# A written-out order of 5993 steps, replaced by another: RWKV-7 attention into a SwiGLU block on one Trainium2 core

## Chip, cores, metric

The kernel runs on one core of one Trainium2 chip. The metric is the device time of one launch in microseconds (us). A core has these engines, each with a queue of its own that it works through in order: TensorE (in the profile PE for matmuls and PEld for the loading of the stationary operand), VectorE (DVE), ScalarE (ACT), GpSimd (POOL; here it mostly issues DMAs) and SyncE (SP; it issues DMAs). Matmuls write to PSUM, and DVE and ACT read it out.

## What is computed

The first half is a recurrence over 768 time steps, for 4 batches of 8 heads with a state of 40 x 40 each; the second half takes its output as 3072 tokens of 320 numbers through a normalisation and a gated feed-forward block with 1536 hidden columns. The feed-forward weights come as 64-bit floats; the kernel works in fp32.

```python
for t in range(S):                                   # S = 768, per batch and head
    y[t] = r[t] @ state
    Sa = state @ a[t]
    state = state * w[t][:, None] - outer(Sa, b[t]) + outer(v[t], k[t])
x = y rearranged to (B*S, H*D)                       # 3072 x 320
xn = x / sqrt(mean(x*x) + 1e-6) * rms_g
g = xn @ w_gate
out = ((g * sigmoid(g)) * (xn @ w_val)) @ w_out
```

## The kernel before

**Stages.** The sequence is cut into 24 chunks of 32 time steps; a chunk is worked on for all 32 batch-heads at once. Each chunk c has three parts, and the feed-forward block has a fourth, for groups of chunks (GROUPS, L21: one chunk, eleven times two, one chunk).

- `front(c)` (L643): loads w, a, k, b and v of the chunk, turns them on PE against the identity (two "turn" steps, L618), and builds, level by level (1, 2, 4, 8, 16), the products of keys with decays. Its PE steps are four "gramk" steps (L683 and, for the levels 4, 8 and 16, L706); between them DVE and ACT prepare the next level's K and Ab. One "turnS" follows.
- `inverse(c)` (L757): solves a triangular system on DVE, with small operations on the tiles Yi and tmp, between two trips through DRAM (sB and sY, issued by SP).
- `main(c)` (L794): PE steps "state", "lower" (two to four), "update", "turn", "turnS", "score", "y0" and five "level" steps, with DVE and ACT between them; then the normalisation with "turn4" and "turn3". It carries the state from chunk to chunk.
- `feed(g)` (L930): for each pair of the 12 slices of the hidden columns, "h64" and "hh" products (gate and value), SiLU on ACT into sg, a multiplication on DVE into hT, and an "out" product into the tile po. The weights come as slices; `narrow` (L964) turns each half slice from 64-bit floats into fp32, with integer and floating operations on DVE and ACT, numbered 0 to 23 in the order of the slices. Slices from the third on are loaded by POOL.

**Operations in the profile.** All operations are recorded by helpers, so the profile's lines are the helpers': L469 is every matmul, L472 every turn on PE, L423 nearly every DVE operation, L450, L453 and L446 the ACT copies, scalings and functions, L466 every DMA, L462 a fill by POOL. What an operation belongs to is read from its tiles' names: `ps` is PSUM but for `po`, `KN` the levels' keys, `As` the scores, `xg` the feed's input, `wf` its weights.

**The order.** The code above does not run in its own order. `Plan.add` (L241) records 5993 steps: 2717 for DVE, 1113 for ACT, 1091 for PE (a step of PE is a whole group of matmuls, for instance the 32 of one "gramk"), 588 for POOL and 484 for SP, each with what it reads and writes. `Plan.issue` (L282) then issues them in one total order, which stands in the literal `ORDER` (L32). Each number there is a distance from the first step not issued yet:

```python
for word in order.split():
    i = first + int(word)
    gone.add(i)
    while first in gone:
        first += 1
```

So the order on each engine's queue is that of its steps in this list. A second literal, `PAIRS` (L185), gives each of 495 "rooms" one of three tiles of PSUM, of two banks each (`ps0` to `ps2`). A room is one use of such a tile, from the first matmul that writes it to the last operation that reads it out (`Plan.room`, L216); a tile is held by one room at a time. The fourth pair of banks, `po`, is not part of this. Before an operation runs, semaphores make it wait for what it needs on other engines; those waits follow from the tiles that it reads and writes.

**Shapes on PE.** A step's stationary operand has rows and columns, which the profile shows as rows*columns in front of the shape of what is moved. The steps differ in them: 128*128 for "hh" and "out", 64*128, 64*104 or 40*128 for "h64" and the turns, 128*40 for "level", 64*64 down to 64*40 for "gramk", "score", "y0" and "update", 64*32 for "state", 32*32 or 16*32 for "lower".

Of the kernel before, what the change touches and what calls it, by code (L numbers as in the profile page):

```python
# [32 lines left out]
76 84 83 86 75 71 2 3 4 5 6 7 0 35 47 0 17 54 64 0 0 51 0 35 0 55 0 0 67 68 60 190 191 41 49 374 59 71 375 0  # L33
35 0 0 0 46 359 380 185 73 0 32 170 171 181 75 74 73 0 1 27 3 0 368 2 0 352 373 343 173 2 167 166 342 72 80 73 85 84 96 69
70 78 83 94 74 365 79 40 53 353 62 371 61 366 354 64 51 52 374 54 81 15 93 75 82 76 92 95 91 367 86 89 90 63 183 77 100 344 168 39
165 297 298 88 104 184 102 106 97 87 105 101 198 108 98 107 348 345 103 185 190 113 99 346 16 656 668 175 176 9 5 31 109 112 368 355 369 116 114 117
115 118 120 119 110 111 347 186 187 122 356 299 359 349 203 370 350 191 657 18 665 4 357 188 197 284 19 17 28 375 121 71 196 376 667 666 43 382 285 377
358 123 202 379 201 213 30 0 401 171 652 41 199 359 379 198 360 25 191 123 300 299 210 124 125 126 127 213 128 211 301 129 192 130 209 203 131 193 132 221
208 206 402 392 654 391 382 390 205 133 207 134 181 657 170 5 194 377 223 219 135 222 136 214 217 137 218 138 204 216 230 393 139 380 225 411 140 141 215 410
413 142 143 226 144 145 383 146 147 148 149 150 151 224 412 234 663 384 235 236 152 385 386 237 168 387 153 155 662 154 156 394 388 403 389 407 395 404 238 239  # L40
240 396 180 414 415 405 406 6 43 318 7 13 433 22 408 398 676 157 432 179 418 399 419 241 416 397 409 229 188 158 159 160 161 400 228 417 452 31 453 244
420 441 443 245 246 434 247 248 444 677 227 242 435 436 243 442 249 220 250 251 252 438 253 254 464 463 169 437 285 454 461 0 460 253 254 437 255 453 284 256
438 456 454 285 286 287 257 482 0 250 251 435 643 447 252 436 449 473 283 280 253 254 281 450 282 255 223 493 256 439 257 258 259 260 261 494 651 437 292 455
438 262 22 662 263 264 440 293 441 456 661 660 1 296 475 457 483 459 479 284 303 458 482 299 460 298 484 285 300 485 461 297 648 665 476 304 302 306 305 222
307 309 477 301 495 310 502 505 650 503 478 664 499 311 221 313 312 266 267 265 268 270 314 504 23 315 486 496 497 763 316 480 271 269 272 764 317 822 821 481
487 498 832 819 676 500 318 488 506 319 490 320 766 544 489 663 501 669 491 507 321 767 322 545 833 768 769 770 536 508 535 829 670 677 323 492 675 682 771 820
525 324 671 772 775 510 680 681 773 692 668 774 534 524 509 325 778 679 678 693 690 688 672 686 765 689 691 673 687 683 779 828 533 16 2 831 827 674 294 699
694 697 511 700 512 526 701 824 830 834 649 823 295 698 702 703 685 527 528 705 684 546 695 782 838 658 0 204 370 380 211 378 203 511 333 205 212 215 206 216
389 390 391 228 467 463 462 460 382 213 381 459 465 464 475 476 214 221 398 222 470 385 383 457 458 388 392 395 393 394 466 461 224 384 469 386 223 217 225 471
450 468 474 752 230 451 226 399 400 401 402 403 404 405 406 407 408 409 410 751 499 249 749 762 759 411 472 412 387 413 473 414 517 250 761 513 415 477 518 416  # L50
417 478 760 418 419 479 420 421 480 422 423 481 424 425 426 427 482 614 615 516 617 510 227 229 509 750 428 629 515 514 396 520 429 431 430 630 432 528 521 397
526 527 522 532 530 529 533 534 523 544 524 531 537 536 541 525 542 538 540 535 543 539 436 434 545 549 553 548 0 553 549 434 545 555 432 550 560 546 554 556
565 566 567 551 558 250 557 230 234 235 518 254 255 231 232 251 617 564 568 571 570 765 615 618 619 233 252 236 559 620 253 770 621 453 569 256 574 771 259 630
257 623 258 260 757 499 575 576 577 578 579 580 581 582 583 584 585 586 587 588 589 590 591 592 593 594 595 596 622 625 624 626 627 597 598 454 746 632 634 633
747 269 764 635 631 0 637 481 0 1 0 478 399 669 679 668 515 558 565 555 516 177 670 556 517 518 519 400 401 181 520 671 178 402 672 564 522 523 521 524
563 562 574 557 477 566 182 179 180 403 567 183 561 568 560 559 573 572 569 570 571 575 576 577 578 579 783 184 844 854 842 841 843 784 682 744 684 685 528 525
526 840 678 852 527 786 683 186 580 187 689 479 404 697 488 407 406 489 696 787 188 788 789 688 690 702 190 849 848 857 405 700 785 713 851 853 839 191 189 701
581 695 790 710 858 791 582 192 850 712 691 583 698 795 584 711 794 724 193 733 709 792 699 847 793 585 692 194 708 798 196 707 693 799 703 195 706 694 723 717
714 719 722 718 704 705 725 715 721 730 0 725 585 715 733 5 196 6 719 734 7 730 726 1 727 736 0 733 6 198 799 0 194 0 547 798 46 799 194 805
0 730 796 543 719 47 728 190 192 803 729 722 798 42 731 799 806 43 44 801 805 48 49 802 795 797 804 50 807 0 763 0 763 689 690 691 692 693 694 695  # L60
767 765 764 766 686 696 768 697 1067 769 803 687 698 770 0 943 942 694 800 766 695 799 767 41 1075 696 802 697 805 1064 698 48 47 813 806 803 1065 1063 1073 699
818 700 817 42 43 0 768 767 1030 657 757 0 4 769 770 784 657 762 5 658 774 0 779 658 762 770 780 775 46 782 791 778 659 781 660 763 776 661 53 52
47 49 54 0 43 759 657 772 784 658 769 659 779 783 788 660 782 661 787 790 662 45 785 664 663 781 50 780 789 791 684 794 665 0 687 746 754 749 639 975
752 753 755 45 0 702 41 424 52 967 42 59 0 572 4 5 710 708 15 382 1 709 384 6 10 7 711 11 383 714 0 10 15 780 11 16 0 573 571 572
570 591 796 799 798 592 780 931 913 717 712 719 713 714 721 715 716 723 718 720 0 0 0 766 781 630 767 914 907 904 631 706 709 710 0 767 905 682 768 0
619 709 710 711 712 713 714 715 716 717 718 719 720 721 722 1 364 894 768 3 769 0 0 1 408 405 341 406 0 356 357 405 358 359 235 311 360 0 414 235
3 360 415 361 236 362 237 363 364 238 365 418 366 367 0 367 428 368 419 394 369 1 430 418 370 238 371 0 0 368 427 0 0 414 418 419 417 421 415 416
423 420 426 430 367 368 543 369 427 431 428 544 545 429 724 370 371 0 431 738 306 432 728 371 538 433 732 434 0 371 434 720 372 538 0 731 434 372 373 0
734 550 537 373 2 376 374 375 377 378 0 718 554 541 2 720 3 542 537 565 727 553 4 725 311 6 547 548 715 730 551 543 312 550 726 552 576 555 563 562
716 560 561 558 723 564 559 7 557 570 544 8 379 9 545 575 380 571 574 13 546 595 378 569 556 566 577 567 568 12 578 584 572 585 582 0 581 9 576 10  # L70
582 5 568 0 568 577 572 383 217 6 579 219 384 569 581 422 578 12 423 220 580 424 654 218 652 425 520 426 653 14 509 655 8 656 585 7 586 587 588 590
589 13 9 591 592 427 593 657 594 595 0 654 591 593 655 594 5 653 10 595 596 597 598 599 600 601 602 603 604 605 606 607 608 609 610 388 658 389 611 577
659 12 578 662 673 663 664 675 668 612 669 665 613 666 667 614 670 671 13 18 14 19 615 676 682 15 20 616 617 618 16 619 620 621 674 672 989 622 677 623
678 680 681 624 679 625 626 982 992 991 979 980 505 981 683 627 628 684 514 629 0 0 0 4 613 668 614 669 615 670 671 616 617 702 706 842 703 575 704 618
619 620 717 707 716 621 709 6 12 722 710 622 624 715 711 623 705 721 719 718 7 733 729 727 744 712 720 731 843 625 728 723 725 730 9 732 713 738 726 13
8 743 14 714 742 737 739 626 734 749 724 10 629 627 745 15 735 639 736 746 748 740 755 747 763 754 756 0 0 962 678 688 741 697 629 742 617 833 661 395
398 397 749 746 748 662 396 747 0 0 657 681 943 954 814 815 658 961 724 829 830 951 828 953 659 626 734 962 671 393 817 0 951 626 817 1 943 398 3 820
# [969 lines left out]
```

## Time and profile before

| what | value |
|---|---|
| median of the runs shown | 1012.67 us (3 runs, 1006.22 to 1016.76) |
| span of the profiled execution | 1021.8 us |
| mean granted TensorE clock over that span | 0.943 |
| HBM read and written | 55.05 MB and 10.22 MB |

The span runs from the first to the last instruction of the profiled execution, and it is that execution's time as far as the profile tells. How to read the lines below: busy time of an engine and its share of the span; "in 40 slices" means tenths of each slice of 25.5 us; a chain is followed back from the last instruction to what released it. A timeline row has the start, the time to the end of the last of its instructions, engine, line, operation, out<-in, rows*columns, shape and count, and in brackets the engine's idle time before it and who ended it. A row of a group has the count, then the busy time in us and the mean of one in ns, then the idle time before them. One fp32 matmul is two records of PE; a turn is one. Ends of matmuls are modelled, so times between steps of PE are taken from start to start.

### The profile page before, as it was taken

What the parts mean: (1) busy time and instruction counts of PE and PEld (TensorE: products, weight loads), DVE (VectorE), ACT (ScalarE), POOL (GpSimd) and SP (SyncE); (2) the same over time, 40 slices, a digit from 0 to 9 for tenths busy, and PEclk for the clock granted to TensorE, in tenths of its full rate; (3) what the DMA queues carried; (4) which work ended last, traced back from release to release, by engine and by line L of the source; (5) the groups of instructions that cost most, each with busy time, mean ns of one, the idle gap of its engine ahead of it and who ended that gap; (6) DMA issues with size and microseconds to landing.
All of it is one profiled execution on the core that took longest, in us unless ns stands there. A gap on an engine that the chain in (4) does not pass through costs nothing.

```text
span 1021.8 us, 55373 instructions
## 1 busy us (share of the span) xinstructions
PE 930.1 (91%) x24512; PEld 759.6 (74%) x24512; DVE 771.4 (75%) x2718; ACT 509.7 (50%) x1133; POOL 350.0 (34%) x595
## 2 busy tenths in 40 slices
PE   4366688999989999999999999999999999999998
PEld 4255577878767787788788777778787878788877
DVE  8889877787867966877769779679598697685531
ACT  6788467445445544465353454454544545435121
POOL 8988363242324314315133143143133224210000
PEclk9557767999999999999999999999999999999999
DMA  8574453323324324133232142242232323320100
GB/s 172 149 190 115 96 110 74 68 47 60 54 58 78 56 53 75 36 71 61 45 81 44 44 95 39 55 84 49 43 72 51 75 50 66 67 35 7 43 8 20
DMA packets 140175, 68.87 MB, mean 67 GB/s; under 512 B 120768, under 2 KB 127264, under 8 KB 139936
## 3 DMA queue, kind: packets, MB, share of 16 engines
q0 software_dynamic: 19680, 32.48, 15.9%
q1 hardware_dynamic: 118080, 32.54, 15.4%
q8 instruction: 192, 3.15, 1.3%
q10 hardware_dynamic: 2176, 0.33, 0.2%
q14 instruction: 47, 0.39, 0.1%
HBM read 55.05 MB, written 10.22 MB: 64 GB/s over the span
## 4 chain that ended last, share of the span: by engine, by line
PE 55%; DVE 24%; DMA 7%; issue 5%; POOL 4%; ACT 3%; SPq 2%; DVEq 0%; ACTq 0%; POOLq 0%
PE ps L469 40%; PE po L469 10%; PE ps L472 5%; DVE Yi L423 4%; DVE LT L423 3%; DVE y L423 3%; DVE tmp L423 3%; DVE K L423 3%; DMA sB<-LT 3%; SPq L466 2%; DVE As L423 2%; DMA M<-sB 2%; DVE Ab L423 1%; POOL wf L466 1%; DVE hT L423 1%
## 5 line engine op out<-in xcount | busy, mean ns | idle before, releaser
L469 PE MATMUL ps<-xg,wf 128*128 128x256 f32 (+3 forms) x1872 | 364.5, 377 | 1.5 <-ACT sg L446 0.8
L469 PEld LDWEIGHTS ps<-xg,wf 128*128 128x128 f32 (+1 forms) x1872 | 271.1, 191 | 48.6 <-issue 8.1
L469 PE MATMUL po<-wf,hT 128*128 128x320 f32 x576 | 179.0, 444 | 0.2 <-issue 0.2
L469 PEld LDWEIGHTS po<-wf,hT 128*128 128x128 f32 x576 | 103.5, 189 | 35.6 <-issue 1.4
L423 DVE TENSOR_TENSOR tmp<-Yi,M 128x24 f32<-128x24 f32 (+21 forms) x512 | 107.2, 209 | 12.1 <-DMA M<-sB 1.6
L423 DVE TENSOR_TENSOR Yi<-Yi,tmp 128x24 f32<-128x24 f32 (+21 forms) x512 | 106.8, 209 | 10.4
L423 DVE TENSOR_TENSOR hT<-ps,sg 128x256 f32<-128x256 f32 (+1 forms) x156 | 60.6, 399 | 63.7 <-PE ps L469 41.4
L446 ACT ACTIVATE sg<-ps 128x256 f32<-128x256 f32 (+1 forms) x156 | 54.5, 368 | 103.3 <-PE ps L469 102.4
L466 POOL DMA_DIRECT2D kbn<-in_k_dram x92 | 53.6, 585 | 146.9 <-PE ps L469 146.2
L466 POOL DMA_DIRECT2D kbn<-in_b_dram x92 | 53.8, 587 | 131.2 <-PE ps L469 130.1
L423 DVE TENSOR_TENSOR K<-K,T 128x256 f32<-128x256 f32 (+1 forms) x191 | 92.8, 499 | 3.7 <-PE ps L469 2.8
L469 PE MATMUL ps<-Ab,K 64*60 64x56 f32 (+2 forms) x4608 | 79.4, 224 | 17.5 <-ACT r L450 4.8
L469 PEld LDWEIGHTS ps<-Ab,K 64*60 64x60 f32 (+2 forms) x4608 | 72.6, 136 | 29.0 <-issue 9.3
L423 DVE SCALAR_TENSOR_TENSOR Yi<-M,Yi 128x31 f32<-128x31 f32 (+6 forms) x228 | 43.2, 243 | 66.7 <-DMA out_dram<-o 23.3
L450 ACT COPY KN<-ps 128x640 f32<-128x640 f32 x95 | 65.6, 692 | 46.7 <-PE ps L472 12.9
L466 POOL DMA_DIRECT2D VU<-in_v_dram x92 | 54.1, 590 | 88.0 <-PE ps L469 86.3
L423 DVE TENSOR_TENSOR As<-ps,msi 128x256 f32<-128x256 f32 (+1 forms) x168 | 70.7, 455 | 11.9 <-PE ps L469 7.0
L469 PEld LDWEIGHTS ps<-As,KN 128*40 128x40 f32 x3072 | 67.3, 128 | 15.2 <-issue 5.3
L469 PE MATMUL ps<-As,KN 128*40 128x32 f32 x3072 | 72.0, 208 | 6.1 <-DVE As L423 2.9
L466 POOL DMA_DIRECT2D wn<-in_w_dram x92 | 52.4, 571 | 69.6 <-DVE KN L423 65.4
L450 ACT COPY K<-K 128x512 f32<-128x512 f32 x95 | 60.2, 634 | 23.7 <-PE ps L469 10.9
L456 POOL TENSOR_TENSOR ss<-ss,mhalf 128x1 f32<-128x1 f32 x24 | 18.1, 755 | 147.1 <-DVE ss L423 146.9
(137 smaller groups left out, 1526.4 us busy)
## 6 DMA issues: line engine op xcount, KB each, us to landing
M<-sB SPq DMA_DIRECT2D x96, 128.0 KB, 2.9
wan<-in_r_dram SPq DMA_DIRECT2D x24, 160.0 KB, 4.2
kbn<-in_b_dram POOLq DMA_DIRECT2D x92, 40.0 KB, 2.5
VU<-in_v_dram POOLq DMA_DIRECT2D x92, 40.0 KB, 2.7
wan<-in_w_dram POOLq DMA_DIRECT2D x46, 80.0 KB, 3.0
wan<-in_a_dram POOLq DMA_DIRECT2D x46, 80.0 KB, 2.8
kbn<-in_k_dram POOLq DMA_DIRECT2D x92, 40.0 KB, 2.7
wn<-in_w_dram POOLq DMA_DIRECT2D x92, 40.0 KB, 2.9
```

Source lines behind the costliest of these rows:

```text
L423: plan.add("DVE", time + more + each * size(o), 0.087, lambda at: [fn(at(o), *m(at))], [o], aps(*args))
L446: scalar(o, [a], lambda at: nc.scalar.activation(at(o), at(a), f, **kw), aps(acc), 0.1 if f in (AF.Square, AF.Relu) else 0.0)
L450: scalar(o, [a], lambda at: nc.scalar.copy(at(o), at(a)), extra=more)
L456: plan.add("POOL", 0.5, 0.06, lambda at: nc.gpsimd.tensor_tensor(o, a, b, op), [o], [a, b])
L466: plan.add(by, 0.6 if by == "POOL" else 0.45, 0.0, lambda at: queue.dma_start(out=o, in_=i), [o], [i], load=load, since=since)
L469: return o, lhsT, rhs, lambda at: nc.tensor.matmul(at(o), lhsT, rhs, start=start, stop=stop, skip_group_check=True), 4
L472: return o, i, ident, lambda at: nc.tensor.transpose(at(o), i, ident), 2
```

## The change

Only the two literals change. Nothing in the code that records or issues steps changes, so the 5993 steps, their instructions, and what they read and write are the same; what differs is the total order of the steps, and which of the three PSUM tiles each room uses.

```diff
 ORDER = """
-76 84 83 86 75 71 2 3 4 5 6 7 0 35 47 0 17 54 64 0 0 51 0 35 0 55 0 0 67 68 60 190 191 41 49 374 59 71 375 0
...
 PAIRS = """
-212020210212120201011000000002122102121202002110201212101120120100121021022021021012211022112120021122201112110120220200
...
-112220222120210
+012020211110110202122012002002221020200121110112220101221201120110010221222020001211121110112102011120212121001220012122
...
+000112121012120
```

Taken as indices into the recorded steps, the two lists compare like this:

| engine | steps | mean shift of a step's place in its queue | largest |
|---|---|---|---|
| PE | 1091 | 3.6 | 25 |
| DVE | 2717 | 7.0 | 175 |
| ACT | 1113 | 5.0 | 37 |
| POOL | 588 | 9.5 | 98 |
| SP | 484 | 3.8 | 35 |

The first nine steps of PE are the same; after them the lists part. Before, PE goes on with the first product of `main(0)`, the four "gramk" of `front(1)`, a turn of `front(2)`, and then the rest of `main(0)`. After, `front(1)` goes first, then `main(0)` up to its first "level" steps, and that turn of `front(2)` stands among them. The feed of group 0 begins with the 90th step of PE before, and with the 93rd after; there, before, the four "gramk" of `front(4)` stand together ahead of it.

More of the change, by code (lines that the diff above doesn't have):

```diff
@@ L32 @@
 ORDER = """
[150 rows of a table removed]
[150 rows of a table added]
 """
 PAIRS = """
-212020210212120201011000000002122102121202002110201212101120120100121021022021021012211022112120021122201112110120220200
-211101012202202011120000200020220222022111222002110010201111111221020101112100110011110120101220200212221202210202000120
-200001010122101111022221020102022012211212111120001012110101122002220000222011120101011110101020010100212121202001201010
-202022202022012001121220211222122020022201202021101121220111201111101001012220112210102111212102000010100200202021210201
-112220222120210
+012020211110110202122012002002221020200121110112220101221201120110010221222020001211121110112102011120212121001220012122
+110000102110020222200202111100101120121200020101000120101022212021211112100022021222222202020002100021000010201201001202
+022111111210120202010201212212202120120212111120101202121010022201010100021122221212022210121000210100200201020112021121
+112011002020100012212101010020201112021112010122010002020121212111000220221001102010221022221102200201020011221211012021
+000112121012120
 """
```

299 rows, old and new, of the table ORDER are left out of this document.

## The prediction

> **What bounds the kernel now.** I read the busy rows and slices first, then stretches of the span, then the chain, then PE's own timeline.
>
> ```profile
> span 1021.8 us, 55373 instructions
> PE 930.1 (91%) x24512; PEld 759.6 (74%) x24512; DVE 771.4 (75%) x2718; ACT 509.7 (50%) x1133; POOL 350.0 (34%) x595
> PE   4366688999989999999999999999999999999998
> DVE  8889877787867966877769779679598697685531
> PE 55%; DVE 24%; DMA 7%; issue 5%; POOL 4%; ACT 3%; SPq 2%; DVEq 0%; ACTq 0%; POOLq 0%
> ```
>
> PE is nearly full from the tenth slice on; in the slices before that DVE is the fuller one. So there are two stages with different limits. The place where one hands over to the other is the last of front(5)'s four level products, the second half of this group:
>
> ```profile
> 192.09 0.28 DVE L423 TENSOR_TENSOR Ab<-Ab,T 128x128 f32<-128x128 f32 x1
> 192.16 1.83 PE L469 MATMUL ps<-Ab,K 64*56 64x56 f32 x128
> ```
>
> The stretches, cut there and finer (PE, PEld, DVE, ACT, POOL busy, then granted clock):
>
> ```profile
> 0.00:50.00 50.00, 20.15 (x672) 18.25 (x672) 44.49 (x138) 33.40 (x60) 44.58 (x83) 0.78 0.72 160
> 50.00:100.00 50.00, 31.93 (x1288) 28.55 (x1288) 44.40 (x127) 41.04 (x78) 44.01 (x71) 0.64 0.64 154
> 100.00:150.00 50.00, 35.53 (x1314) 32.22 (x1315) 41.51 (x138) 29.51 (x62) 23.45 (x40) 0.64 0.47 105
> 150.00:200.00 50.00, 45.07 (x1445) 39.34 (x1429) 39.15 (x129) 30.26 (x70) 16.86 (x29) 0.89 0.34 66
> 0.00:193.20 193.20, 125.90 (x4541) 112.65 (x4545) 166.23 (x521) 131.59 (x262) 126.62 (x217) 0.73 0.55 123
> 193.20:1022.00 828.80, 804.24 (x19989) 646.93 (x19978) 605.15 (x2197) 378.10 (x871) 223.39 (x378) 0.99 0.28 54
> ```
>
> The reader is to see: in the first 193.20 us DVE works 166.23, PE only 125.90. In the other 828.80 us PE works 804.24, and DVE has 223 us of slack. So the time is, nearly, DVE's work ahead of the handover plus PE's work behind it, plus 27.0 us of idle DVE in the first stretch and 24.6 us of idle PE in the second. An order changes the two sums only by moving steps across the handover and by changing what PE loses between steps; the rest of its effect is in the 27.0 and the 24.6.
>
> **The change, part by part.** No instruction is added or removed; I took each number of the two lists as an index into the 5993 steps, and counted.
>
> *Changes of shape.* By shape I mean a stationary operand's rows*columns, each rounded up to 32, 64 or 128. The old list has 487 changes of shape between matmuls that follow each other, the new one 471. Behind the handover: 422 against 408, of which 156 against 144 enter 128*128 (hh and out), 155 against 143 leave it, and 111 against 121 are others. So 12 visits to 128*128 fewer, 10 other changes more. Their price is in PE's timeline:
>
> ```profile
> 403.30 1.13 PE L469 MATMUL ps<-xg,wf 128*128 128x256 f32 x4
> 404.36 0.78 PE L469 MATMUL ps<-ST,aP 64*32 64x40 f32 x64
> 416.74 0.20 PE L469 MATMUL ps<-r,Sd 64*40 64x32 f32 x2
> 416.76 0.20 PE L469 MATMUL ps<-rE,Sd 64*40 64x32 f32 x1
> 416.89 0.54 PE L469 MATMUL po<-wf,hT 128*128 128x320 f32 x1
> 447.03 3.72 PE L469 MATMUL ps<-xg,wf 128*128 128x256 f32 x16
> 450.68 0.79 PE L469 MATMUL ps<-Xs,LT 32*32 32x40 f32 x64
> ```
>
> One hh step (x4) holds PE from 403.30 to 404.36, 1.06 us; four in a row from 447.03 to 450.68, 3.65. So a further step costs (3.65 - 1.06) / 3 = 0.863 and the visit itself 1.06 - 0.863 = 0.197. To that comes the entry: 416.76 to 416.89 is 0.13, where matmuls of one shape follow after 0.02; 0.11 more. A visit costs 0.31 us, another change about 0.11 (I take the entry gap for it). Sum: -12 x 0.31 + 10 x 0.11 = -2.6 us. The lower end is nothing where PE would have stood still anyway, 24.6 of 828.8, so 3% of it; the upper is -3.7 if the ten others cost nothing. The two changes saved ahead of the handover count as nothing: DVE covers them. Cover gone, they cost two times 0.11.
>
> The Trainium skill, in TensorEngine Tiling (Array Packing), Key Properties, says that a change of tiling mode, not of tile alone, drains the engine. By that rule alone all changes cost alike: -14 x 0.11 = -1.5 us. The rows agree that a change costs, and differ in that a visit to 128*128 costs more than two gaps (0.31 against 0.22); I go by the rows.
>
> *Steps moved over the handover, DVE.* 516 of DVE's steps stood up to the one that releases that product, now 513. Out go three of narrow 23, KN2 of front(4) and one T; in come one hT and one Yi.
>
> ```profile
> L423 DVE TENSOR_SCALAR o<-exs 128x480 int32<-128x480 int32 x2 | 0.8, 402 | 0.0
> L423 DVE TENSOR_SCALAR exs<-exs 128x480 int32<-128x480 int32 x2 | 0.8, 398 | 0.0
> L423 DVE SCALAR_TENSOR_TENSOR exs<-exs 128x480 f32<-128x480 uint32 x2 | 1.3, 646 | 0.0
> L423 DVE TENSOR_TENSOR KN<-kbn,wn 128x640 f32<-128x640 f32 x24 | 19.7, 821 | 0.8 <-issue 0.5
> L423 DVE TENSOR_TENSOR T<-T 128x16 f32<-128x16 f32 x22 | 3.7, 168 | 0.1
> L423 DVE TENSOR_TENSOR hT<-ps,sg 128x128 f32<-128x128 f32 x24 | 6.5, 288 | 24.6 <-PE ps L469 15.1 <-ACT sg L446 8.1 <-PE po L469 1.4
> L423 DVE TENSOR_TENSOR Yi<-Yi,tmp 128x8 f32<-128x8 f32 x24 | 4.1, 169 | 0.2
> ```
>
> 0.402 + 0.398 + 0.646 + 0.821 + 0.168 - 0.288 - 0.169 = 2.0 us less. What is put off runs in DVE's slack behind the handover; without that slack it would cost the same 2.0 there. Ends: 0 if the moved steps only make idle time, and the 27.0 us of idle DVE either way if the stage packs better or worse.
>
> *Steps moved over the handover, PE.* One: the update of main(3), behind it before, now ahead, where PE is idle a third of the time. Its like:
>
> ```profile
> 430.45 0.83 PE L469 MATMUL ps<-VU,KN 64*40 64x40 f32 x64
> 431.22 0.75 PE L472 MATMUL ps<-ident,kbn 64*104 64x64 f32 x16
> ```
>
> 430.45 to 431.22, less one exit gap of 0.13: -0.64 us. If DVE did not cover it there, it would cost the same 0.64.
>
> *The queues.* On POOL, the loads for front(2)'s second turn now end with the 93rd of POOL's steps, not the 77th; on PE that turn is 23rd, not 16th.
>
> ```profile
> 50.69 1.10 PE L472 MATMUL ps<-ident,kbn 64*104 64x64 f32 x16 [8.25 <-POOL kbn L462]
> 86.09 1.97 PE L469 MATMUL ps<-A,K 64*64 64x56 f32 x64
> L466 POOL DMA_DIRECT2D kbn<-in_k_dram x92 | 53.6, 585 | 146.9 <-PE ps L469 146.2
> ```
>
> Sixteen steps at 0.585 make 9.4 us later; what reads that turn's result first is PE's product at 86.09, 35 us after it, so I cost it at nothing; with the cover gone it would be 9.4. Behind that turn on PE stood, idle for 8.25 us, the work of chunk 0; in the new list seven of these steps go first. SP's 484 loads shift by 3.8 places in the mean, and SP's queue has 2% of the chain: nothing, at most that 2%, 20 us, either way.
>
> *PSUM pairs.* Behind the handover 113 of 413 rooms followed their pair's last writing step after less than 2 us of PE work; now 135 of 412. Price nothing, since PE's idle time there is small; its end is in the second rival.
>
> **Sum.** -2.6 - 2.0 - 0.6 = -5.2 us: 1016.6 against the profiled 1021.8. The runs shown have a median of 1012.67 (1006.22 to 1016.76), 0.9% under the profiled span; scaled, 1007.5 us. Bounds of these terms alone: 1003 to 1012. About 1%, 10 us, is what a measurement of this kernel can tell from no change.
>
> **The rivals.**
>
> *Faster: chunk 0 no longer stands behind that turn.* All 8.25 us go on to the end: 1007.5 - 8.2 = 999.3. It decides (over 1%) from 5 us of the 8.25. For it: only 137 instead of 205 of DVE's steps stand ahead of main(1)'s first product. Against it: DVE, which bounds this stage, was busy 44.40 of those 50 us, so there were 5.6 us to win there, and steps that come sooner in one place come later in another.
>
> *Slower: the PSUM pairs come round too soon.* 22 more rooms have less than 2 us of cover. A reader that empties a pair takes
>
> ```profile
> L450 ACT COPY KN<-ps 128x640 f32<-128x640 f32 x95 | 65.6, 692 | 46.7 <-PE ps L472 12.9
> ```
>
> and if PE waits out such a copy in each, 22 x 0.692 = 15.2 us: 1007.5 + 15.2 = 1022.7. It passes 1% from 0.7 us each. Against it: the 113 of before cannot have cost over 24.6 us in all, 0.22 each, and 22 x 0.22 is 4.8, still within 1%. For it: PE has no slack behind the handover, so a wait of any kind there shows whole.
>
> *Slower: the granted clock.* It was 0.64 in 50:150 and 0.89 in 150:200. If the new order leaves PE's first-stage work in thinner groups and the clock stays at half, the work of 150:200 grows by 45.07 x (0.89 / 0.5 - 1) = 35 us; with half of it on the path, 1007.5 + 17 = 1025. Against it: DVE's work up to the handover and PE's are as before, to 2 us and one step, so PE is as dense there as it was. The Trainium skill, in TensorE: Matmul & The Clock Gate, Part 1, has the clock at half until a window of steady work lets it up; 0.64 between 50 and 150 and 0.99 behind 193 agree.
>
> *The change does little of what it says.* 16 changes fewer of 487 is 3%. That is in the forecast: even at 0.31 us each they would be worth 5 us.
>
> **How the numbers follow.** The forecast, within 1%, gets 0.44. Both sums are counted, but 52 us of idle time that a new order deals out anew are not. Faster gets 0.30: one place with a long wait is visibly mended, in a stage with little to win. Slower by PSUM gets 0.22, by the clock 0.04. So faster 0.30, same 0.44, slower 0.26. The likeliest gives 1007.5, its own range 1002 to 1013; the range for 8 in 10 takes in 999 with as much again of the idle 27 (988) and 1022.7 to 1025: 988 to 1026.
>
> **What would show it.** Right: PE behind the handover busy some 2 to 4 us less, DVE about 164 us ahead of front(5)'s last product, that product near 191, PE's idle time behind it near 25 us. The first wait of 8.25 us on POOL's kbn gone or short. Wrong: the handover off by over 8 us (the first stage packs otherwise), or idle PE behind it over 35 or under 15 us. A single hh visit not near 1.06 us against 0.863 for a further step would make the price wrong.

## The result, and the profile after

| | median | runs | ratio to before |
|---|---|---|---|
| before | 1011.76 us | 4 runs, 1006.22 to 1016.76 | |
| after | 1037.79 us | 4 runs, 1034.85 to 1045.08 | 1.0267, 95% interval 1.0215 to 1.0320 |

The change makes the kernel 26 us slower. 1007.5 was forecast, and 988 to 1026 as the range: the time lies outside it. The profiled execution of before (span 1021.8) lies 1% above its median, that of after (1034.5) a little under its own, so the two profiles differ by 12.7 us only; a second profiled execution of before, below, has 1017.4.

The page of after, the lines that answer to those of before:

```profile
span 1034.5 us, 55331 instructions
PE 926.7 (90%) x24512; PEld 765.0 (74%) x24512; DVE 781.9 (76%) x2718; ACT 509.2 (49%) x1133; POOL 346.0 (33%) x595
PE   5356678999999998999989999899999999999998
DVE  8987977786877886868878778688687787686541
PE 67%; DVE 11%; issue 8%; DMA 5%; ACT 4%; POOL 3%; SPq 2%; DVEq 0%; POOLq 0%; ACTq 0%
```

PE's busy time fell by 3.4 us, and yet the span grew. In the chain, "issue" (time in which an engine waits for nothing that the profile shows) went from 5% to 8%, and PE's slices show eights where before had nines. The stretches, cut at the handover of after (the last gramk of front(5), now at 195.64):

```profile
0.00:195.70 195.70, 125.52 (x4594) 112.43 (x4598) 167.39 (x517) 130.64 (x258) 120.84 (x214) 0.73 0.53 122
195.70:1034.00 838.30, 801.14 (x19936) 652.58 (x19924) 614.56 (x2203) 378.51 (x875) 225.18 (x381) 0.99 0.27 54
```

Behind the handover PE works 801.14 us, 3.1 less than in the first profile of before, as forecast; but the second profile of before has 801.52, so two executions of one kernel differ by as much:

```profile
193.20:1017.40 824.20, 801.52 (x20010) 644.91 (x20001) 605.54 (x2198) 378.50 (x871) 223.38 (x378) 1.00 0.28 55
```

What grew is the time in which PE stands idle there: 838.30 - 801.14 = 37.2 us, where before has 24.6. What it waits for is in the waits of PE from 196 us on (us in all, times, longest), first before, then after:

```profile
PE ps L469 <- issue: 6.4, 8, 2.3
```

```profile
PE ps L469 <- issue: 23.6, 27, 1.8
PE ps L469 <- DMA LT<-sY: 4.2, 3, 2.9
PE ps L472 <- issue: 2.4, 2, 1.7
```

So in 29 of its waits, 26.0 of the 37.2 us, no operand, no PSUM tile and no engine is late as far as the profile shows. PE's waits for other engines even became fewer: all that stand in the same list with ACT or DVE as the releaser come to 10.0 us before and to 2.2 after. Two of the 29 places in the timeline of after, the updates of main(9) and main(10):

```profile
440.31 1.33 PE L469 MATMUL ps<-Ab,K 64*56 64x56 f32 x92
441.46 0.31 PE L469 MATMUL ps<-VU,KN 64*40 64x40 f32 x11
443.37 0.73 PE L469 MATMUL ps<-VU,KN 64*40 64x40 f32 x53 [1.60 <-issue]
444.03 1.34 PE L469 MATMUL po<-wf,hT 128*128 128x320 f32 x4
445.31 1.13 PE L469 MATMUL ps<-xg,wf 64*128 64x256 f32 x8
...
479.60 2.86 PE L469 MATMUL ps<-xg,wf 128*128 128x256 f32 x12
482.39 1.83 PE L469 MATMUL ps<-Ab,K 64*56 64x56 f32 x128
484.04 0.31 PE L469 MATMUL ps<-VU,KN 64*40 64x40 f32 x10
486.20 0.74 PE L469 MATMUL ps<-VU,KN 64*40 64x40 f32 x54 [1.85 <-issue]
```

The update of main(9) is the row at 430.45 that the prediction quoted from before: 0.77 us to the next step there, 444.03 - 441.46 = 2.57 here. The pause cuts the step in two, after 11 of 64 records in one place and 10 in the other.

Counting PE's instructions from its first (each matmul record, each weight load, each semaphore event as one), the pause at 443.37 stands ahead of number 84 x 256 + 193. So do most others: behind the handover 29 gaps in which no matmul runs are over 0.35 us, and 24 of them lie at 192 or 193 beyond a multiple of 256, 24.7 of 29.7 us. Counted from one matmul's start to the next (over 0.35 us, less 0.1 us each for the matmul itself), 36 lie at 190 to 197, 32.0 us in all; before it is 15 with 9.8 us. This second count is the one used below. The page shows what has that period. This row of the DMA queues is the same before and after:

```profile
q8 instruction: 192, 3.15, 1.3%
```

3.15 MB in 192 packets, 16 KB each, for 24512 + 24512 matmuls and loads: 255 a packet. The runs below, which add instructions to PE alone, have one packet more for every 256 of them (193 in e5 with 24640 matmuls, 194 in e17 with 24782; 35 in e4 with 4480). So PE's instructions come by DMA, in blocks of 256.

### The profile page after: what moved, and what is told of

The parts are those of the page before. It is cut to its first block, busy times and chain, and to the rows that moved or that the text cites. A ratio compares the mean times of both kernels' runs of the same rounds, so it can differ in the third digit from the quotient of the medians.

```text
span 1034.5 us, 55331 instructions
## 1 busy us (share of the span) xinstructions
PE 926.7 (90%) x24512; PEld 765.0 (74%) x24512; DVE 781.9 (76%) x2718; ACT 509.2 (49%) x1133; POOL 346.0 (33%) x595
## 3 DMA queue, kind: packets, MB, share of 16 engines
q8 instruction: 192, 3.15, 1.3%
## 4 chain that ended last, share of the span: by engine, by line
PE 67%; DVE 11%; issue 8%; DMA 5%; ACT 4%; POOL 3%; SPq 2%; DVEq 0%; POOLq 0%; ACTq 0%
PE ps L469 49%; PE po L469 13%; PE ps L472 6%; SPq L466 2%; DVE y L423 2%; DVE Yi L423 1%; DVE tmp L423 1%; DMA wf<-in_moe_w_out_dram 1%; ACT VU L450 1%; DVE As L423 1%; DVE LT L423 1%; DVE K L423 1%; DMA sB<-LT 1%; DVE wf L423 1%; DMA LT<-sY 1%
## 5 line engine op out<-in xcount | busy, mean ns | idle before, releaser
L469 PEld LDWEIGHTS po<-wf,hT 128*128 128x128 f32 x576 | 105.9, 193 | 37.7 <-issue 3.4
L450 ACT COPY K<-K 128x512 f32<-128x512 f32 x95 | 60.3, 635 | 31.2 <-PE ps L469 14.1
L423 DVE SCALAR_TENSOR_TENSOR Yi<-M,Yi 128x31 f32<-128x31 f32 (+7 forms) x228 | 46.1, 244 | 36.4 <-DMA M<-sB 17.1
```

The costliest lines, as they stand in the source:

```text
L423: plan.add("DVE", time + more + each * size(o), 0.087, lambda at: [fn(at(o), *m(at))], [o], aps(*args))
L450: scalar(o, [a], lambda at: nc.scalar.copy(at(o), at(a)), extra=more)
L469: return o, lhsT, rhs, lambda at: nc.tensor.matmul(at(o), lhsT, rhs, start=start, stop=stop, skip_group_check=True), 4
```

## The experiments

**Theory F:** at each cut between two blocks PE stands still unless the block before took long enough, some 3.3 us. Steps of small matmuls in a row (gramk, gramk, update; state, lower, lower) use up 256 instructions in 1.5 to 2 us. Whether a cut falls behind such a run is settled by the number of instructions ahead of it, which the forecast did not look at; the change moved the cuts. **Rival O:** the new order has waits of its own between steps, and "issue" is only their name. Behind each ratio below (4 to 12 runs each) stands its 95% interval; "+ 256" is 256 more instructions of PE; "issue" is the sum of PE's waits of that name over the whole span, from the profile.

| kernel | ratio to before | issue, us (times) | span |
|---|---|---|---|
| before, first and second profile | | 10.4 (14), 10.5 (12) | 1021.8, 1017.4 |
| before + 256 ahead (e5) | 1.0013 (0.998 to 1.0046) | 9.9 (12) | 1021.7 |
| before + 176 ahead (e1) | 1.0245 (1.0191 to 1.030) | 28.0 (35) | 1035.4 |
| before + 96 ahead (e2) | 1.0287 (1.0253 to 1.0321) | 39.4 (41) | 1048.9 |
| before + 176 at 230 us (e9) | 1.0267 (1.0225 to 1.0309) | 31.2 (34) | 1044.0 |
| before + 256 at 230 us (e10) | 1.0051 (1.0021 to 1.0082) | 6.5 (11) | 1019.2 |
| the same, own outputs (e18) | 1.0042 (1.0014 to 1.007) | 8.6 (10) | 1016.3 |
| before + 32 at 800 us (e12) | 1.0000 (0.9973 to 1.0028) | 6.7 (11) | 1015.1 |
| before, feed steps spread (e7) | 1.0109 (1.0074 to 1.0143) | 9.9 (13) | 1032.2 |
| after | 1.0267 (1.0215 to 1.032) | 33.9 (38) | 1034.5 |
| after + 96 ahead (e3) | 1.0275 (1.0218 to 1.0331) | 34.3 (31) | 1038.7 |
| after, feed steps spread (e6) | 1.0292 (1.0228 to 1.0355) | 22.4 (28) | 1047.0 |
| after, cuts moved at 2 places (e11) | 1.0204 (1.0163 to 1.0246) | 20.1 (28) | 1032.5 |
| at 9 places (e13) | 1.0220 (1.0182 to 1.0258) | 17.3 (21) | 1034.7 |
| at 12 places (e14) | 1.0201 (1.0158 to 1.0244) | 25.2 (24) | 1040.0 |
| at 7 places behind the handover (e15) | 1.0213 (1.0158 to 1.0269) | 22.3 (24) | 1034.4 |
| at the 2 early places alone (e16) | 1.0314 (1.0263 to 1.0364) | 33.7 (39) | 1042.5 |
| at 6 places, own outputs (e17) | 1.0147 (1.0104 to 1.0191) | 20.1 (21) | 1026.8 |

### The same order, all cuts shifted

Small matmuls on zeros are issued ahead of everything, 4 PE instructions each: 44 (e1), 24 (e2, and e3 on after), 64 (e5, one whole block). No step is moved.

```diff
+    pad = const.tile([P, 32], FP32, name="pad")
+    nc.vector.memset(pad, 0.0)
     with tc.manual_schedule():
+        for _ in range(44):
+            nc.tensor.matmul(po_[0:32, 0, 0:32], pad, pad, start=True, stop=True, skip_group_check=True)
         plan.issue(ORDER, PAIRS)
```

> The order and the PSUM pairs of before, with 44 small matmuls (176 instructions of PE) put ahead of everything, where PE stands idle anyway (its first matmul of before starts at 5.71 us). Theory F (PE's instructions come in blocks of 256, by the 192 fetches of 16 KB that the DMA rows show, and no block can pass faster than about 3.3 us): only the places where the blocks begin move, by 176. Counted over the order behind the handover, the blocks that are too short lack 14.5 us in before and 36.6 us here, so this is slower by 15 to 24 us. Rival O (the new order is slower by its own waits, for PSUM pairs or between stages): same as before, within 3 us.

> As the run with 176, with 24 matmuls (96 instructions). Theory F: the short blocks lack 29.0 us in place of 14.5, so slower than before by 10 to 16 us, less than with 176. Rival O: same as before, within 3 us.

> The changed kernel, with 24 small matmuls (96 instructions of PE) ahead of everything. Theory F: the short blocks lack 24.8 us in place of 36.4, so 8 to 12 us faster than the changed kernel, near 1027 us. Rival O: as the changed kernel, near 1038 us.

> Order and pairs of before; 64 small matmuls (256 PE instructions) ahead of everything. F: the cuts between blocks of 256 instructions fall on the same steps as in before, so PE stands still behind the handover about as long as there (9.8 us, at 15 places), and the time is that of before, +0 to +6 us. O, and any rule by which padding itself costs: +20 to +30 us, as with 176 and 96 instructions of padding.

Measured: 176 instructions cost 25 us, 96 cost 30, and 256, the most work of the three, nothing. That is F, and O can't explain it: the order is that of before in all three. The dose was missed, 96 came out dearer than 176 (its handover came at 200.6 instead of 193.0 us, which the reckoning of the blocks leaves out). On after, 96 were to bring 8 to 12 us and brought nothing: the pauses behind the handover fell from 32.0 to 24.3 us by the count above, those ahead of it rose from 12.3 to 15.2, and PE's waits for the DMA LT<-sY behind the handover rose from 4.2 to 10.1.

### The blocks by themselves

e4 leaves out the whole computation and writes a constant. PE does 64 large products (128*128), 1024 small ones in a row (64*60, 56 columns, as in gramk), 64 large ones, and then as many small and large ones mixed, 32 and 2 in turn.

```python
large(wide, 64)
for _ in range(32):
    small(dense)        # 32 products
large(late, 64)
for _ in range(32):
    small(mixed)
    large(wmix, 2)
```

> Leaves out the whole computation; the output holds a constant. Measures the price by itself: 1024 small matmuls (64*60 stationary, 56 columns) in one run without another shape, then 64 large ones (128*128, 256 columns), then the same 1024 and 64 mixed, 32 small and 2 large in turn. Theory F: the run of small ones has 4096 instructions, 16 blocks, so 16 x 3.3 = 53 us though their work is 32 x 0.62 = 20 us; grouped, with the large ones behind, some 53 + 28 = 81 us; mixed 55 to 65 us, because the large ones run while the next block comes, although the mixed part has 63 changes of shape more. Rival S (changes of shape are the price that counts, PE takes instructions as fast as it works): grouped 48 us, mixed 48 + 32 x 0.31 = 58 us.

The timeline of e4, the row before the first cut, three blocks of the small ones, the first of the large ones after them, and the start and end of the mixed part:

```profile
32.47 3.29 PE L33 MATMUL dense<-x,w 64*60 64x56 f32 x223
36.97 1.98 PE L33 MATMUL dense<-x,w 64*60 64x56 f32 x128 [1.21 <-issue]
40.42 1.98 PE L33 MATMUL dense<-x,w 64*60 64x56 f32 x128 [1.48 <-issue]
43.88 1.98 PE L33 MATMUL dense<-x,w 64*60 64x56 f32 x128 [1.48 <-issue]
...
87.29 27.89 PE L38 MATMUL late<-x,w 128*128 128x256 f32 x128
115.12 1.10 PE L33 MATMUL mixed<-x,w 64*60 64x56 f32 x64
116.15 1.13 PE L38 MATMUL wmix<-x,w 128*128 128x256 f32 x4
...
181.02 1.13 PE L38 MATMUL wmix<-x,w 128*128 128x256 f32 x4
```

128 records and their 128 loads, 256 instructions, keep PE for 1.98 us, and the next 128 start 3.45 us after them, block upon block. (Here there is nothing else on any engine.) Small and large together take 115.12 - 32.47 = 82.65 us when grouped by shape and, by the end of the last row, 182.15 - 115.12 = 67.0 us mixed, with 63 changes of shape inside it where the grouped part has one. So an order that saves changes of shape by grouping loses 15.6 us here, and PE does not take instructions as fast as it could work (the expectation's rival S, 48 us grouped). The mixed part came out 2 us above what F expected; the price of the changes of shape is a likely reason, not shown apart.

The Trainium skill, in Runtime: NRT & Kernel Launch, Instruction fetch mechanics, says that instructions come in blocks of 256, the next one being fetched while the present one is executed, and that crossing from one to the next is mostly hidden. The blocks agree with the trace; "hidden" does not, for small fp32 matmuls in a row: in e4, 1.48 us of every 3.45 is the crossing.

The lists of DMA packets show what a pause waits for. In each of the 20 traces there are as many 16 KB packets as cuts, and, packets and cuts taken in turn, no cut is passed earlier than 1.15 us after the end of the packet for the block behind it. A packet takes about 1.1 us. About half of them start 0.6 to 1.2 us after the cut before, and about one in ten ahead of that cut.

### Moving the steps instead of the cuts

e6 moves 32 feed steps of after, e7 20 of before, by at most four places on PE, so that the dense runs are broken up. One line of ORDER of e7 (the distance 8 goes to a later place):

```diff
-13 12 7 8 381 555 382 570 581 383 575 579 384 583 385 578 565 386 387 388 582 580 584 9 14 586 576 587
+13 12 7 381 555 382 570 581 383 575 579 384 583 385 578 565 386 387 388 582 580 584 9 14 586 8 576 587
```

> Order of after with 32 feed steps (20 hh, 7 out, 5 h64) moved by at most four places on PE, behind the handover, so that gramk, gramk, update or state, lower, lower no longer fall into one block of 256 instructions; PAIRS of after. By nominal durations the lack of the blocks against 3.3 us falls from 37.7 to about 14.5 us, and 2.9 us of shape changes are added. F: about 20 us faster than after, 1014 to 1022 us where before takes 1015. O: the waits of the new order stay, no faster than 1033 us.

> Order of before with 20 feed steps (10 hh, 8 out, 2 h64) moved by at most four places on PE, behind the handover; PAIRS of before. By nominal durations the lack of the blocks against 3.3 us falls from 16 to about 2 us, and 1.7 us of shape changes are added. F: 5 to 10 us faster than before, since before stands still 9.8 us at the starts of blocks there. O: nothing gained, 0 to +5 us by the shape changes.

> The kernel before, unchanged, for a second profiled execution. F: PE stands still at the same places again (398, 727, 784 us from the start) and some 10 us in all behind the handover. O: the standstills are chance and lie elsewhere.

In e6 "issue" falls from 33.9 to 22.4 us as meant, and yet it is no faster than after; e7 is 1.1% slower than before, with "issue" unchanged. Here F failed as a recipe: from 196 us on PE's waits for ACT and DVE rose, to 17.9 us in e6 where after has 2.2, and to 16.3 in e7 where the two profiles of before have 10.0 and 10.2. An order whose feed steps cover waits can't have them moved for free. (In e7's profile the handover also came at 198.05 us, 5 later than in before, though every moved step stands behind it; that isn't explained.) e8 shows that the pauses of before are not chance: its longest stand at 394 and 724 us, in the steps where the first profile has them at 398 and 727, with 10.5 us of "issue" in all against 10.4.

### The cuts moved at one place, the start untouched

One step issues its first matmul again and again, which changes nothing in its result. In e9 it is 44 times in the last gramk of front(6), in e10 64 times, a whole block.

```diff
+AGAIN = {1632: 44}
...
     def pe(kind, steps, more=[]):
+        again = AGAIN.get(len(plan.pieces), 0)
+
         def issue(at):
-            return [s[3](at) for s in steps]
+            return [s[3](at) for s in steps[:1] * again + steps]
```

> Order and pairs of before; in the last gramk of front(6), about 230 us from the start, the first matmul is repeated 44 times (176 PE instructions, 1.1 us by the mean of one); everything ahead of it is unchanged. By nominal durations the lack of the blocks of 256 instructions against 3.3 us rises behind it from 15.6 to 38.6 us. F: 10 to 22 us slower than before, about as slow as after, with the handover at 193 us as before and the time lost behind 230 us. O: slower by the 1.1 us of the repeated matmuls, at most 2 us.

> As the run with 44 repeats, with 64 (256 PE instructions, 1.6 us): the cuts between blocks fall on the same matmuls as in before, and the lack stays at 15.6 us. F: 0 to 4 us slower than before, though more work is added than in the run with 44. O: a little slower than the run with 44 repeats.

PE's waits of the name in e9, then in e10 (lines stand three further on: L472 is every matmul, L475 every turn):

```profile
PE ps L472 <- issue: 25.0, 24, 2.1
PE ps L475 <- issue: 6.0, 9, 1.2
PE po L472 <- issue: 0.2, 1, 0.2
```

```profile
PE ps L472 <- issue: 5.7, 9, 2.1
PE ps L475 <- issue: 0.4, 1, 0.4
PE po L472 <- issue: 0.4, 1, 0.4
```

This is the sharpest pair: the same order, 1.0267 with 44 repeats, 1.0051 with 64. One place with 176 more instructions makes of before a kernel as slow as after; 80 further instructions undo it. O falls as the whole explanation.

e10's repeats were reckoned at 1.6 us, and it is 5 us slower than before. The last two gramk of front(6) in e10, the second with the repeats, and the same two steps in e5, which has none:

```profile
234.41 8.08 PE L472 MATMUL ps<-Ab,K 64*56 64x56 f32 x256 [0.34 <-DVE LT L426]
242.42 1.13 PE L472 MATMUL ps<-xg,wf 128*128 128x256 f32 x4
```

```profile
237.56 1.83 PE L469 MATMUL ps<-Ab,K 64*56 64x56 f32 x128 [0.33 <-DVE LT L423]
239.32 1.13 PE L469 MATMUL ps<-xg,wf 128*128 128x256 f32 x4
```

Start to start it is 8.01 us against 1.76: 6.25 / 64 = 98 ns for each repeat, and not the 25 ns (0.80 us for 32) that the expectation took. e18 issues the step's own 32 matmuls twice more instead, each on its own output.

> As the run of before with 64 repeats in the last gramk of front(6), but its 32 matmuls are issued twice more, each on its own outputs. F: 1.6 us of work and the cuts between blocks as in before: 1.000 to 1.003 times before, less than with the repeats of one matmul (1.0051). O: the same as with those.

The same two steps in the timeline of e18, to the start of the next one:

```profile
234.19 2.47 PE L472 MATMUL ps<-Ab,K 64*56 64x56 f32 x179 [0.33 <-DVE LT L426]
237.77 1.19 PE L472 MATMUL ps<-Ab,K 64*48 64x56 f32 x77 [1.10 <-issue]
238.89 1.13 PE L472 MATMUL ps<-xg,wf 128*128 128x256 f32 x4
```

4.70 us, of which 1.10 a pause at a cut: (4.70 - 1.10 - 1.76) / 64 = 29 ns each. In the whole time e18 and e10 can't be told apart (1.0042, 1.0051); the price of a repeat is shown by these rows alone.

### After, with its cuts moved

The same edit on after, with the places chosen so that the dense runs end before a cut: `AGAIN = {2197: 24, 3738: 44}` in e11, nine places in e13, twelve in e14. e12 is the same on before, `{5075: 8}`.

> Order and pairs of after; the first matmul is repeated 24 times in the state of main(7) and 44 times in a gramk of front(15) (272 PE instructions, 1.5 us), no step is moved. By nominal durations the lack of the blocks falls from 38.2 to 18.0 us. F: standstills at the starts of blocks behind the handover fall from 32 to about 14 us; half of that comes back as other waits, as in the run with spread feed steps, so 8 to 18 us faster than after, 1.005 to 1.018 times before. O: after's own waits stay, no faster than after (1.027 times before).

> Order and pairs of before; the first matmul of one lower step of main(19) is repeated 8 times (32 PE instructions, 0.15 us), no step is moved. By nominal durations the lack of the blocks behind it falls by 4.7 us, from 15.6 to 10.9. F: 0 to 4 us faster than before. O: the same time.

> Order and pairs of after; in nine steps (update of main(1), lower of main(2), state of main(4), (7), (9), (11) and (13), a level of main(12), update of main(19)) the first matmul is repeated 3 to 27 times, 135 times in all (540 PE instructions, 2.6 us), no step is moved. The places are chosen from the trace of after: with its standstills at block starts taken out, the lack of the blocks against 3.0 us is 27.0 us as it stands and 8.2 us with the repeats (before by the same count: 7.3). F: standstills at block starts fall from 44 us (whole span) to about 15 to 20, and the time is 1.000 to 1.012 times before. O (after's order has some 15 us of waits of its own): 1.018 times before or more.

> As the run with nine steps, but the places are chosen against a lack of 3.2 us: twelve steps, 134 repeats (2.6 us). The lack against 3.2 us falls from 35.5 to 11.1 us (before 10.4). F: 1.000 to 1.012 times before, and within 0.5% of the run with nine steps. O: 1.018 times before or more.

e12 gained nothing that can be measured. e11 gained 6 us against after, less than expected, and e13 and e14 no more, though "issue" fell by up to half. Two reasons were tried. First, the handover (the start of front(5)'s last gramk), in the timeline of after, then of e13:

```profile
195.64 0.22 PE L469 MATMUL ps<-Ab,K 64*48 64x56 f32 x1
```

```profile
205.22 0.25 PE L472 MATMUL ps<-Ab,K 64*48 64x56 f32 x3
```

The stretch behind it had shrunk from 833.8 to 824.5 us (first start of the gramk to PE's last step), and 9.6 us were lost ahead of it. e15 leaves out the two early places (their repeats go to the state of main(4)), e16 keeps only them.

> As the run with nine steps, without its two places ahead of the handover; their 49 repeats stand in the state of main(4) instead, so that every cut between blocks behind the handover lies where it lay in that run, and everything ahead of it is as in after. In the run with nine steps the stretch behind the handover fell from 833.8 to 824.5 us and the handover itself came at 205.2 instead of 195.6 us. F: handover near 195.6, behind it about 824 us, so 1.004 to 1.014 times before. O: the handover is early again but the stretch behind it is 830 us or more; 1.018 or more.

> Only the two places ahead of the handover (22 repeats in the update of main(1), 27 in the lower of main(2)) and 15 in the state of main(4), 256 PE instructions in all, so that behind the handover the cuts lie as in after. If the two places delayed the handover in the run with nine steps: handover near 205 us, behind it 834 us, 1.030 to 1.040 times before. If that delay was chance of one execution: handover 194 to 198 us and the time of after, 1.022 to 1.030.

The same row in e16, then in e15:

```profile
203.85 0.25 PE L472 MATMUL ps<-Ab,K 64*48 64x56 f32 x3
```

```profile
196.16 0.22 PE L472 MATMUL ps<-Ab,K 64*48 64x56 f32 x1
```

So it was the two early places that delayed the handover, by some 8 us. But e15, with the start in order again, was no faster: behind the handover it took 833.3 us, which spoke for O. Second reason: the repeats. They were reckoned at 2.6 us in all, but in e15 116 of the 135 stand in state, where each took 72 ns (the five state steps with repeats take 11.86 us from start to start, and one without takes 0.71), and behind the handover PE was busy 808.19 us, 7.0 more than in after. That is half of the account: PE's "issue" waits from 196 us on had fallen by 13.0 us (26.0 to 13.0), and its waits for LT<-sY had risen by 5.2 (4.2 to 9.4). e17 repeats other steps' own matmuls, at six places, none of them ahead of the handover.

```diff
+AGAIN = {1449: 49, 1951: 27, 2430: 16, 3388: 10, 3867: 18, 5080: 15}
...
-            return [s[3](at) for s in steps]
+            return [s[3](at) for s in (steps * 2)[:again] + steps]
```

> Order and pairs of after; in six steps behind the handover (update of main(4) and main(19), y0 of main(6), (8), (12) and (14)) the first 10 to 49 matmuls of the step are issued once more ahead of it, 135 in all, each on its own outputs and not one and the same again and again, since the repeats of one matmul took 54 to 62 ns each and not 25. Nothing ahead of the handover differs from after. The lack against 3.0 us falls from 27.0 to 10.4 us, for 2.6 us of work. F: handover 194 to 198 us, standstills behind it 10 to 17 us instead of 32, the stretch behind it 820 to 828 us, 1.004 to 1.015 times before. O: other waits take the place of the standstills, the stretch stays at 830 us or more, 1.018 or more.

(The 54 to 62 ns in it are not what the rows give: 98 in gramk, 72 in state.) Its update of main(9) in the timeline, and PE's waits over the span:

```profile
436.47 0.82 PE L472 MATMUL ps<-VU,KN 64*40 64x40 f32 x64
437.22 1.34 PE L472 MATMUL po<-wf,hT 128*128 128x320 f32 x4
```

```profile
PE ps L472 <- issue: 16.3, 16, 2.5
PE ps L475 <- issue: 3.8, 5, 1.4
```

The step is whole again and takes 0.75 us, and the kernel is at 1.0147 (1.0104 to 1.0191), with the handover at 195.17 and 826.6 us behind it: as F expected; O's 830 us or more for that stretch is missed, though the interval of the ratio reaches its 1.018. Nearly half of the change's loss is gone, with after's order and pairs as they are and 135 matmuls added. It is no version that beats before.

**What the table says.** Over the 17 profiled executions other than e6 and e7, span = 1012.0 + 0.90 x "issue" fits with a correlation of 0.93 (single executions, on different chips; the worst lies 8 us off, and it is that of after). After has 23.5 us of "issue" more than before, so by this line 21 of the 26 us go with it. The shifts of before (e1, e9 against e5, e10) show the cause; that 21 us of after's loss are of this kind is a reading of the line, and e17 shows 12 of them. What stays open: no run brought after below 20 us of "issue" with the start undisturbed, so whether its order, without any pause, would equal before's isn't shown. O is right in part: behind the handover PE waits 4.2 to 10.1 us for LT<-sY in every run on after's order, and at most 2.5 in every run on before's, and these waits grew when pauses went (from 4.2 to 7.3 us in e17).

## Why the prediction was wrong, point by point

**The frame.** "DVE's work ahead of the handover plus PE's work behind it" plus idle time held; what failed is in the idle time. The prediction's own sign of being wrong came: over 35 us of idle PE behind the handover, 37.2.

**Changes of shape, -2.6.** The price of a visit holds in after: three hh steps in a row, 479.60 to 482.39, are 2.79 us, and 0.197 + 3 x 0.863 = 2.79 by the forecast's terms. The gain itself isn't shown: PE's busy time behind the handover is 804.24 us in the first profile of before, 801.52 in the second and 801.14 in after, and the clock was at half there for 3.4 us at three, one and four places, so a difference of 3 us can't be put down to the change. At best it was a gain of 2.6 beside a loss of ten times that.

**DVE moved over the handover, -2.0.** Not borne out. The handover came 2.6 us later (195.64, before 193.03), not 2 earlier, and 195.2 to 196.2 in e11, e15 and e17, which are like after up to there. DVE was busy 167.39 us ahead of it, not 164; but to the same time it is 164.71 in e15 and 168.05 in e17, so 2 us can't be told here. What made the handover later wasn't tried. **The update moved ahead, -0.6,** can't be seen beside this.

**"An order changes the two sums only by moving steps across the handover and by changing what PE loses between steps."** This is the step that failed. PE also loses time inside steps, by where the cuts between blocks of 256 instructions fall: 26.0 of the 37.2 us behind the handover in after are waits of that kind, 7.2 of the 24.6 in before. Any change of order or of the number of instructions moves all cuts behind it. The forecast took the whole 24.6 as waits that a new order deals out anew, and put nothing for the cuts; before is a favourable case of them (by luck or not, no run shows). Taking out the pauses from the second profile of before and shifting the cuts by 16, 32, ... 240 instructions, the blocks behind the handover lack some 8 to 22 us against 3.0 us each, and some 7 as they stand; that e1 and e2 are slower bears it out, though not the order of the two. After has 23 to 27 by that count (it depends on what is taken out as a pause), and no shift of the whole brings it under 16. It could have been read: "issue" was 5% of before's chain, and its timeline has this, in the middle of the last gramk of a front, with its data at hand (timeline of before; the first row holds the gramk before it and 38 records of the last):

```profile
394.66 1.56 PE L469 MATMUL ps<-Ab,K 64*56 64x56 f32 x102
398.53 0.59 PE L469 MATMUL ps<-Ab,K 64*48 64x56 f32 x26 [2.30 <-issue]
```

A pause that no releaser explains wants an explanation of its own, before a sum is made without it.

**The rivals.** *Chunk 0 behind front(2)'s turn:* the wait is gone, as the diff let expect, and it brought nothing, as was argued against it (timeline of after):

```profile
70.31 1.10 PE L472 MATMUL ps<-ident,kbn 64*104 64x64 f32 x16
```

*PSUM pairs:* not the cause of what is read here. PE's waits for ACT and DVE, which empty the pairs, fell to 2.2 us behind the handover, and e9 loses as much with the old pairs; no run has the new order with the old pairs. The forecast gave "slower" 0.26, most of it for this reason, so the sign was among the cases and the mechanism in none. *The clock:* 0.73 ahead of the handover and 0.99 behind it, as before. *Little of what it says:* the shape changes were worth too little to be seen.

## What to carry to other kernels

On a kernel that is near full on TensorE with many small fp32 matmuls, look for "issue" waits of PE that cut a step in two, and reckon PE's instructions in blocks: a run of 256 that takes under about 3.3 us can end in a pause of up to 2 us if a cut falls behind it. Any edit ahead of such runs, however small, moves the cuts and can be worth 2.5% by itself, so before a change is judged, a control belongs to it that shifts the cuts alone (some dozens of matmuls ahead, and then a whole block's worth). Grouping small steps by shape, to save changes of tile, makes the dense runs longer (e4).

## What the runs showed of the hardware that was not expected

- **In a row of small fp32 matmuls PE's instructions come no faster than 256 in 3.45 us** (e4), 13.5 ns each, while the matmuls could take 256 in 1.98. That is the transfer's start after the cut (1.04 us behind 36.97), its 1.05 us, and 1.36 from its end to the next cut. A single block can be shorter: nine blocks of before pass in 2.0 to 2.6 us, each behind one of over 4 us. In some places the transfer starts some 5 us after the cut (387.2 and 716.8 us in the second profile of before, each with a pause at the next cut), though the DMA engines were busy by 0.24 and 0.50 there; why stays open.
- **After a pause the clock can fall.** It doesn't after each. In after PE pauses up to 410.17; the window 410.70:414.10 has the clock at half, and eight records of "out" take 4.02 us from start to start (410.73 to 414.75), where four took 1.28 in the rows above (444.03 to 445.31). Before has the same behind the pause up to 398.53, which is clock 0.50 from 399.8 to 403.0. The timeline and the window of after:

```profile
410.17 0.63 PE L469 MATMUL ps<-Xs,LT 32*32 32x40 f32 x47 [1.65 <-issue]
410.73 4.09 PE L469 MATMUL po<-wf,hT 128*128 128x320 f32 x8
414.75 0.66 PE L472 MATMUL ps<-ident,VU 64*104 64x64 f32 x16
```

```profile
410.70:414.10 3.40, 3.40 (x18) 2.19 (x8) 3.09 (x17) 3.15 (x10) 3.02 (x6) 0.50 0.22 42
```

- **Repeating one matmul on its own output costs 98 ns in gramk and 72 in state;** issuing the gramk's matmuls in turn, each on its own output, costs 29 (e10, e15, e18).
